# A chunked-attention and feed-forward kernel on one core: whole weight blocks staged in later weights' places, rests formed by TensorE, the first tile in one pass, and values and scores in one block

## The chip, the core and the metric

The kernel runs on one core of a Trainium2 chip. A core has five engines with an instruction queue each: PE (TensorE, matrix products, with its weight loads shown apart as PEld), DVE (VectorE), ACT (ScalarE), POOL (GpSimd) and SP (SyncE, which here only issues DMAs). Each queue runs strictly in the order in which the program emits instructions. Semaphores make one engine wait for another. The metric is the device time of one launch in microseconds (us); lower is better.

## What is computed

Eight batches of 576 tokens, eight heads of 64. Attention stays inside chunks of 64 tokens; then a normalised feed-forward block (FFN) with 2048 hidden units is added to its own input.

```python
scores = scale * np.matmul(q_c, k_c.transpose(0, 1, 2, 4, 3))     # chunks of 64
scores = scores - np.max(scores, axis=-1, keepdims=True)
attn = np.exp(scores); attn = attn / (np.sum(attn, axis=-1, keepdims=True) + 1e-09)
out = np.matmul(attn, v_c)                                         # -> x, 4608 tokens x 512
xn = (x - mu) / np.sqrt(var + 1e-06) * g_ln
ch = np.maximum(xn @ w_ch1, 0.0) @ w_ch2
return (x + ch).astype(np.float32)
```

The two FFN weight matrices come in as float64 and are converted on the chip.

## The kernel before

**Tiles and blocks.** The 4608 tokens are 18 pairs of 256 tokens, and 9 tiles of two pairs. The hidden units are 16 blocks f of 128. A block's weights are 128x1024: 512 columns for the first matrix and 512 rows of the second. For near-float32 accuracy every operand is held as a high part in the one-pass format fp32r (names ending in h) and a rest (names ending in l), and every product is three matmuls: high by high, high by rest, rest by high. `up(f)` (L287) is 12 matmuls 128x512 into the PSUM tile h for a whole tile (128x256 for a single pair); `split(f, h)` (L300) lets ACT form hh (L304) and DVE hl (L305); `down(f)` (L310) is 12 matmuls 128x512 for a tile (6 for a pair) that add into the four PSUM banks y. `finish` (L322) scales y, adds x (DVE, L326) and stores.

**Weight conversion.** `convert_w` (L116) runs over 32 half blocks of 512 columns. `fetch_w` (L78) loads a half block as 64-bit words (512 KB) into one of three buffers. `start_w` (L85) takes the absolute value of the high words into wf (ACT, L89). `round_w` (L92) packs float64 into float32 bits by four DVE instructions (L96, L97, L100, L104) and lets ACT round the result to the high part wh (L108). `split_w` (L110) forms the rest wl on DVE (L113), after which the buffer takes the next half.

**Attention of a pair** (L132): q and k by DMA, 64 small score matmuls (L159), row maxima (DVE, L166), subtraction (DVE, L172) and exponential (ACT, L176) into p_sb, transposes of p_sb, the sums of the rows (DVE, L182 to L184), 64 small value matmuls (L216), division into x (DVE, L224), mean and variance (L234, L235), xg (L239), transposes of xg, and the split of the transposed xg into xth and xtl. The pairs of the first two tiles do their transposes on PE (L191, L255), with ACT copying pt_sb and xth out of PSUM (L193, L256) and DVE forming xtl (L248). Later pairs transpose on DVE (L204, L267), with ACT forming xth (L270) and POOL forming xtl (L248).

**Order.** Everything above is a generator; a string names, letter by letter, which one takes its next step, and the engines' queues follow that order. START: a, b, A, B are the attentions of the pairs of tiles 0 and 1, C, D and E those of tile 2 and of the first pair of tile 3, w the conversion, and u/1, v/2, x/3, s/4 the products and splits of four single pairs (tiles 0 and 1) over blocks 0 to 5; y/5 and z/6 run blocks 6 to 15 of tiles 0 and 1 at full width. Then STEADY is played once for each of tiles 2 to 7 (FFN of one tile, u/1, beside the attention of the next one's pairs, A from its third step and B) and LAST for tile 8. In STEADY every block of 64 score or 64 value matmuls stands alone between FFN products. PSUM has eight banks: two for attention (`ps_a`), two for h, four for y.

Of the kernel before, what the change touches and what calls it, by code (L numbers as in the profile page):

```python
# [30 lines left out]
RAW_AHEAD = 3  # L31
# [4 lines left out]
START = "aawawaawawabwabAawawaabbwawaubbuwb11buwubu1BuAb1AAuwuAb1buwbAbAwvA2vAv2Auv1BwA2vvCu2vwBvu2vvwB12vAvB2AABBx3BwxBx3xBx3xB3xBwBBxx3x3CxDswxs34ws4sssw4s4sssw4w4swy5s4wyy5yw5ywyy5yywy5yyw5yw5ywC5yyw5wyCzCyw5C6yyzzC5CC6EzCC6CCzCCDzzz6zCD6Dzz6DDzD6zzDzzDD6DD6zzDzDD6z6D"  # L36

FIRST_FFNS = [("u1", 0, 0, 1, 0, 6), ("v2", 0, 1, 1, 0, 6), ("x3", 1, 0, 1, 0, 6), ("s4", 1, 1, 1, 0, 6), ("y5", 0, 0, 2, 6, 16), ("z6", 1, 0, 2, 6, 16)]
STEADY = "Au1ABu1AuAu1AuAu1AuAu1AuAu1AuAu1AuAu1AuBu1BEuBu1BuBu1BuBu1BuBu1BuBu1BuBu1BuBu1uu1"
LAST = "u1u1uu1uu1uu1uu1uu1uu1uu1uu1uu1uu1uu1uu1uu1uu1uu1"  # L40
# [10 lines left out]
def chunk_attention_ffn(ctx: ExitStack, tc: tile.TileContext, qkv, g, w, out):  # L51
# [10 lines left out]
    raw_pool = ctx.enter_context(tc.tile_pool(name="raws", bufs=RAW_AHEAD))  # L62
    ps_a = ctx.enter_context(tc.tile_pool(name="ps_a", bufs=2, space=PSUM))
# [4 lines left out]
    make_identity(nc, ident)  # L68
    mhalf = const.tile([P, 2], F32, name="mhalf")
# [3 lines left out]
    wh = [const.tile([P, NW], F32R, name=f"wh{i}") for i in range(NF)]  # L73
    wl = [const.tile([P, NW], F32R, name=f"wl{i}") for i in range(NF)]

    stage, converted = {}, set()

    def fetch_w(i):  # L78
        if i < 2 * NF:
            raw = raw_pool.tile([P, HALF], U64, name="raw")  # L80
            nc.sync.dma_start(raw, w[i // 2, :, (i % 2) * HALF : (i % 2 + 1) * HALF])
            words = raw.bitcast(U32).rearrange("p (n two) -> p n two", two=2)
            stage[i] = words[:, :, 0], words[:, :, 1]

    def start_w(i):  # L85
        if i < 2 * NF:
            lo, hi = stage[i]
            wf = raw_pool.tile([P, HALF], F32, name="wf", bufs=1)
            nc.scalar.activation(wf, hi.bitcast(F32), AF.Abs)  # L89
            stage[i] = lo, hi, wf  # L90

    def round_w(i):  # L92
# [10 lines left out]
        start_w(i + 1)  # L103
# [3 lines left out]
        f, cs = i // 2, slice((i % 2) * HALF, (i % 2 + 1) * HALF)  # L107
        nc.scalar.copy(wh[f][:, cs], lo.bitcast(F32))  # L108

    def split_w(i):  # L110
        wf = stage.pop(i)[0].bitcast(F32)
        f, cs = i // 2, slice((i % 2) * HALF, (i % 2 + 1) * HALF)
        nc.vector.tensor_tensor(out=wl[f][:, cs], in0=wf, in1=wh[f][:, cs].bitcast(F32), op=ALU.subtract)  # L113
        converted.add(i)

    def convert_w():  # L116

        for i in range(RAW_AHEAD):
            fetch_w(i)
        yield  # L120
        start_w(0)
        yield
        for i in range(2 * NF):
            round_w(i)
            if i > 0:
                split_w(i - 1)
                fetch_w(i - 1 + RAW_AHEAD)
            yield
        split_w(2 * NF - 1)
        yield  # L130

    def attention(pair, xt_cols, xs, by_pe):  # L132
# [8 lines left out]
        top = small.tile([P, 2 * HP, 2], F32, name="top")  # L141
        den = small.tile([P, 2 * HP, 2], F32, name="den")
        rden = small.tile([P, 2 * HP, 2], F32, name="rden")
        p_sb = work.tile([P, 2 * HP, 2, D], F32, name="p_sb", tag="work")

        def bank():
            return ps_a.tile([P, DM], F32, name="s")

        def rows(bank_):
            return bank_.rearrange("p (a d) -> p a d", d=D)  # L150

        s = [rows(bank()) for _ in range(2)]
# [10 lines left out]
        if by_pe:  # L163
            yield
        for h2 in range(2):
            nc.vector.tensor_reduce(out=top[:, :, h2], in_=s[h2], axis=AX.X, op=ALU.max)  # L166
# [4 lines left out]
        for h2 in range(2):  # L171
            nc.vector.tensor_tensor(  # L172
                out=p_sb[:, :, h2, :], in0=s[h2], in1=top[:, :, h2 : h2 + 1].broadcast_to([P, 2 * HP, D]),
                op=ALU.subtract,
            )
            nc.scalar.activation(p_sb[:, :, h2, :], p_sb[:, :, h2, :], AF.Exp, scale=scale)  # L176
            if by_pe and h2 == 0:
                yield
        yield

        def denominators():
            nc.vector.tensor_reduce(out=den, in_=p_sb, axis=AX.X, op=ALU.add)  # L182
            nc.vector.tensor_scalar_add(den, den, 1e-9)
            nc.vector.reciprocal(rden, den)  # L184


        pt_sb = work.tile([P, 2 * HP, 2, D], F32, name="pt_sb", tag="work")
        if by_pe:
            pt = [bank().rearrange("p (a t) -> p a t", a=HP) for _ in range(2)]
            for a in range(2 * HP):  # L190
                nc.tensor.transpose(out=pt[a // HP][:, a % HP, :], in_=p_sb[:, a, :, :], identity=ident)  # L191
            for j in range(2):
                nc.scalar.copy(  # L193
                    pt_sb[:, j * HP : (j + 1) * HP], pt[j].rearrange("p a (c t) -> p a c t", c=2)
                )
            yield
            denominators()
            yield
        else:
# [8 lines left out]
            denominators()  # L208

        o = [rows(bank()) for _ in range(2)]  # L210
        for j in range(2):
            for a in range(HP):
                for h2 in range(2):
                    r = slice(h2 * D, (h2 + 1) * D)
                    for c in range(2):
                        nc.tensor.matmul(  # L216
                            o[h2][c * D : (c + 1) * D, j * HP + a, :], lhsT=pt_sb[r, j * HP + a, c, :],
                            rhs=v_t[j][r, a, c, :], start=True, stop=True,
                        )
        yield  # L220
        x = keep.tile([P, 2, DM], F32, name="x")
        x_h = x.rearrange("p j (a b d) -> p (j a) b d", a=HP, b=2)
        for h2 in range(2):
            nc.vector.tensor_tensor(  # L224
                out=x_h[:, :, h2, :], in0=o[h2], in1=rden[:, :, h2 : h2 + 1].broadcast_to([P, 2 * HP, D]),
                op=ALU.mult,
            )
        yield
# [16 lines left out]

        def rest(on, j, xt):
            js = slice(j * P, (j + 1) * P)
            on.tensor_tensor(out=xtl[:, :, js], in0=xt, in1=xth[:, :, js].bitcast(F32), op=ALU.subtract)  # L248

        if by_pe:  # L250
            xt = []
            for j in range(2):
                xt.append(bank().rearrange("p (k t) -> p k t", k=NK))
                for k in range(NK):
                    nc.tensor.transpose(out=xt[j][:, k, :], in_=xg[:, j, k * P : (k + 1) * P], identity=ident)  # L255
                nc.scalar.copy(xth[:, :, j * P : (j + 1) * P], xt[j])  # L256
                if j == 0:
                    yield
                    rest(nc.vector, 0, xt[0])
            yield  # L260
            rest(nc.vector, 1, xt[1])
        else:
# [6 lines left out]
            for j in range(2):  # L269
                nc.scalar.copy(xth[:, :, j * P : (j + 1) * P], xt[:, j * NK : (j + 1) * NK, :])  # L270
                rest(nc.gpsimd, j, xt[:, j * NK : (j + 1) * NK, :])
# [7 lines left out]
    def ffn(first, n, xt, xs, fs, last):  # L279

        nt = n * PAIR
        slots = DM // nt
        held = []
        f0, f1 = fs
        y = []

        def up(f):  # L287
            assert 2 * f in converted and all(first + i in xs for i in range(n))
# [3 lines left out]
            for k in range(NK):  # L292
                for wx, x in ((wh, xth), (wh, xtl), (wl, xth)):
                    nc.tensor.matmul(  # L294
                        h, lhsT=wx[f][:, k * P : (k + 1) * P], rhs=x[:, k, :], start=m == 0, stop=m == 3 * NK - 1
                    )
                    m += 1
            return h

        def split(f, h):  # L300
            if f % slots == 0:
                held[:] = [hp_.tile([P, slots, nt], F32R, name=f"h{i}") for i in "hl"]
            hh, hl = (x[:, f % slots, :] for x in held)
# [4 lines left out]
            return hh, hl  # L308

        def down(f, hh, hl):  # L310
            assert 2 * f + 1 in converted
            if f == f0:
                y.extend(ps_y.tile([P, DM], F32, name="y") for _ in range(2 * n))
            for j in range(2 * n):
                js = slice(j * P, (j + 1) * P)
                for m, (hx, wx) in enumerate(((hh, wh), (hh, wl), (hl, wh))):
                    nc.tensor.matmul(  # L317
                        y[j], lhsT=hx[:, js], rhs=wx[f][:, DM:],
                        start=f == f0 and m == 0, stop=f == f1 - 1 and m == 2,
                    )  # L320

        def finish():  # L322
            for j in range(2 * n):
                pair, jj = first + j // 2, j % 2
                x, rstd = xs[pair]
                nc.vector.scalar_tensor_tensor(  # L326
# [104 lines left out]
```

## Time and profile before

| | us |
|---|---|
| median of 3 runs | 898.54 (897.41 to 898.60) |
| profiled execution | 899.33 |
| its span on the core | 897.60 |
| granted TensorE clock | 0.997 |
| busy: PE, DVE, ACT | 853.5, 568.3, 173.3 |

The span is what the instruction rows cover; the profiled execution's own time is 1.73 us longer, and 0.79 us above the median of the runs. In all rows the first number of a timeline or chain line is the start in us from the beginning of the span and the second its duration. Matmuls overlap, so the distance between the starts of two neighbours is what one costs, not the duration that its row shows. The chain of waits goes backwards from the last instruction and names at each step what was waited for.

### The profile page before, as it was taken

To read this page: it belongs to the slowest core of one execution; us is meant where nothing else is said; L and a number is where in the kernel's file an instruction comes from. 1 tells how busy PE (TensorE), PEld (TensorE's weight loads), DVE (VectorE), ACT (ScalarE), POOL (GpSimd) and SP (SyncE) were. 2 spreads that over 40 slices of the span, in tenths; PEclk is the share of its full clock that TensorE was granted. 3 is DMA by queue.
4 is the path that set the end of the run, shared out by engine and by line. 5 is a ranking of instruction groups with operands and counts; after the bars stand their busy time and mean duration, and the time that the engine had idled before them with its cause. 6 is when DMAs were issued, how large, how long until landed. Compare 5 with 4: busy or idle time off the path is not lost.

```text
span 897.6 us, 14036 instructions
## 1 busy us (share of the span) xinstructions
PE 853.5 (95%) x5968; PEld 706.5 (79%) x5968; DVE 568.3 (63%) x1104; ACT 173.3 (19%) x301; POOL 48.3 (5%) x53
## 2 busy tenths in 40 slices
PE   2379999999999999999999999999999999999998
PEld 2368888888888788878888888888888888888886
DVE  5988887788876566656565656565666565661112
ACT  3343433412111111121212021212011111111110
POOL 0000000001000000010101010101010101010000
PEclk9999999999999999999999999999999999999999
DMA  6544153212030103010301030103010220000001
GB/s 220 191 145 161 62 175 118 94 48 71 1 135 8 48 0 119 24 47 1 119 24 47 1 118 24 47 1 117 25 47 1 72 71 1 1 30 19 0 1 47
DMA packets 20367, 55.70 MB, mean 62 GB/s; under 512 B 2256, under 2 KB 2256, under 8 KB 20304
## 3 DMA queue, kind: packets, MB, share of 16 engines
q1 hardware_dynamic: 20160, 54.53, 17.4%
q8 instruction: 47, 0.77, 0.4%
q10 hardware_dynamic: 144, 0.26, 0.1%
q14 instruction: 16, 0.13, 0.0%
HBM read 45.35 MB, written 9.44 MB: 61 GB/s over the span
## 4 chain that ended last, share of the span: by engine, by line
PE 89%; DVE 6%; DMA 2%; ACT 1%; issue 1%; SPq 0%; DVEq 0%; ACTq 0%
PE h L294 44%; PE y L317 41%; PE s L159 2%; PE s L216 2%; DMA k_t<-qkv 1%; DVE pt_sb L204 1%; DMA raw<-w 1%; DVE raw L100 1%; DVE raw L104 1%; DVE x L326 1%; DVE hl L305 1%; ACT hh L304 1%; DVE wf L97 0%; DVE top L166 0%; DVE wl L113 0%
## 5 line engine op out<-in xcount | busy, mean ns | idle before, releaser
L305 DVE SCALAR_TENSOR_TENSOR hl<-h,hh 128x512 fp32r<-128x512 f32 (+1 forms) x156 | 101.2, 650 | 264.8 <-ACT hh L304 264.6
L294 PE MATMUL h<-xth,wh 128*128 128x512 f32 (+1 forms) x624 | 236.6, 379 | 0.7 <-ACT xth L256 0.7
L294 PE MATMUL h<-xth,wl 128*128 128x512 f32 (+1 forms) x624 | 233.9, 375 | 3.0 <-DVE wl L113 3.0
L294 PE MATMUL h<-xtl,wh 128*128 128x512 f32 (+1 forms) x624 | 234.0, 375 | 1.1 <-DVE xtl L248 1.1
L317 PE MATMUL y<-wh,hh 128*128 128x512 f32 x576 | 226.0, 392 | 2.1 <-ACT hh L304 2.0
L317 PE MATMUL y<-wl,hh 128*128 128x512 f32 x576 | 224.4, 390 | 0.0
L317 PE MATMUL y<-wh,hl 128*128 128x512 f32 x576 | 224.4, 390 | 0.0
L304 ACT ACTIVATE hh<-h 128x512 fp32r<-128x512 f32 (+1 forms) x156 | 87.8, 564 | 582.5 <-PE h L294 578.9
L294 PEld LDWEIGHTS h<-xth,wl 128*128 128x128 f32 x624 | 118.6, 190 | 23.9 <-DVE wl L113 3.2
L294 PEld LDWEIGHTS h<-xth,wh 128*128 128x128 f32 x624 | 118.5, 190 | 23.2 <-ACT xth L256 1.1
L294 PEld LDWEIGHTS h<-xtl,wh 128*128 128x128 f32 x624 | 118.5, 190 | 22.0 <-DVE xtl L248 1.4
L317 PEld LDWEIGHTS y<-wh,hh 128*128 128x128 f32 x576 | 108.2, 188 | 25.1 <-ACT hh L304 3.0
L317 PEld LDWEIGHTS y<-wh,hl 128*128 128x128 f32 x576 | 108.1, 188 | 23.4 <-DVE hl L305 0.9
L317 PEld LDWEIGHTS y<-wl,hh 128*128 128x128 f32 x576 | 108.2, 188 | 21.5
L204 DVE STREAM_TRANSPOSE pt_sb<-p_sb 32x256 f32<-32x256 f32 x224 | 97.7, 436 | 5.2 <-ACT p_sb L176 1.4
L267 DVE STREAM_TRANSPOSE xt<-xg 32x256 f32<-32x256 f32 x224 | 97.6, 436 | 3.5
L248 POOL TENSOR_TENSOR xtl<-xt,xth 128x512 fp32r<-128x512 f32 x28 | 35.6, 1290 | 644.8 <-ACT xth L270 416.0
L326 DVE SCALAR_TENSOR_TENSOR x<-y,rstd,x 128x512 f32<-128x512 f32 x44 | 30.6, 749 | 15.3 <-PE y L317 15.2
L166 DVE TENSOR_REDUCE top<-s 128x8 f32<-128x512 f32 x36 | 23.2, 686 | 24.4 <-PE s L159 24.4
L89 ACT ACTIVATE wf<-raw 128x512 f32<-128x512 f32 x32 | 21.8, 683 | 76.5 <-DMA raw<-w 53.8
L159 PE MATMUL s<-k_t,q_t 64*64 64x64 f32 x1152 | 22.6, 231 | 14.1 <-DMA k_t<-qkv 14.1
L159 PEld LDWEIGHTS s<-k_t,q_t 64*64 64x64 f32 x1152 | 20.0, 144 | 19.2 <-issue 11.1
(35 smaller groups left out, 383.7 us busy)
## 6 DMA issues: line engine op xcount, KB each, us to landing
raw<-w SPq DMA_DIRECT2D x32, 512.0 KB, 3.6
q_t<-qkv SPq DMA_DIRECT2D x18, 512.0 KB, 4.2
k_t<-qkv SPq DMA_DIRECT2D x18, 512.0 KB, 5.4
v_t<-qkv SPq DMA_DIRECT2D x36, 256.0 KB, 3.1
out<-x SPq DMA_DIRECT2D x36, 256.0 KB, 2.1
g_sb<-g ACTq DMA_DIRECT2D x1, 256.0 KB, 4.5
```

The costliest lines, as they stand in the source:

```text
L89: nc.scalar.activation(wf, hi.bitcast(F32), AF.Abs)
L159: nc.tensor.matmul(s[h2][c * D : (c + 1) * D, j * HP + a, :], lhsT=q_t[r, a, cs], rhs=k_t[r, a, cs], start=True, stop=True,)
L166: nc.vector.tensor_reduce(out=top[:, :, h2], in_=s[h2], axis=AX.X, op=ALU.max)
L204: nc.vector.transpose(out=pt_sb[quad(2 * h2 + j), :, c, quad(i)], in_=p_sb[quad(2 * c + i), :, h2, quad(j)])
L216: nc.tensor.matmul(o[h2][c * D : (c + 1) * D, j * HP + a, :], lhsT=pt_sb[r, j * HP + a, c, :], rhs=v_t[j][r, a, c, :], start=True, stop=True,)
L248: on.tensor_tensor(out=xtl[:, :, js], in0=xt, in1=xth[:, :, js].bitcast(F32), op=ALU.subtract)
L267: nc.vector.transpose(out=xt[quad(j), :, quad(i)], in_=xg[quad(i), :, quad(j)])
L294: nc.tensor.matmul(h, lhsT=wx[f][:, k * P : (k + 1) * P], rhs=x[:, k, :], start=m == 0, stop=m == 3 * NK - 1)
L304: nc.scalar.activation(hh, h, AF.Relu)
L305: nc.vector.scalar_tensor_tensor(out=hl, in0=h, scalar=0.0, in1=hh.bitcast(F32), op0=ALU.max, op1=ALU.subtract)
L317: nc.tensor.matmul(y[j], lhsT=hx[:, js], rhs=wx[f][:, DM:], start=f == f0 and m == 0, stop=f == f1 - 1 and m == 2,)
L326: nc.vector.scalar_tensor_tensor(out=x[:, jj, :], in0=y[j], scalar=rstd[:, jj : jj + 1], in1=x[:, jj, :], op0=ALU.mult, op1=ALU.add)
```

## The change

- Weights: 17 units in place of 32. Block 0 is still converted in halves (units 0 and 1), every other block as a whole (1024 columns, 1 MB by DMA). A whole block needs a bigger buffer: three of them serve, one of its own (`raw`) and the places in which the converted weights of blocks 14 and 15 will stand (`places`). The packing is cut in three steps (`round_w`, `split_w` of the unit before, `sign_w`). For the first four units (blocks 0 to 2) the rest is formed by TensorE: identity times the float32 value plus minus-identity times the high part, in y banks that are still unused, copied out by ACT.
- Attention: the two banks of `ps_a` are one tile; maxima, subtraction, exponential and division each become one instruction over 1024 columns. Pairs a and b get the sums of their rows from TensorE (64 one-column matmuls among the value matmuls, L275 of the new kernel). For the first two tiles the rest xtl is minus-identity times xth added onto the transposes in PSUM, copied by ACT. For later pairs the value products go to the two h banks instead.
- Order: the first tile is finished before the second begins its FFN. Pairs 0 and 1 run blocks 0 to 5 singly, then tile 0 runs blocks 6 to 15. STEADY is played for tiles 1 to 7. In STEADY the values of one pair and the scores of the next stand together (`AB` and `BE` in the string), at two places for a tile; `ROOM = (3, 11)` names the blocks before which no further `up` is emitted, so that both h banks are free for the values there. In the last tile the last two blocks' `down` are ordered by bank of y.

The core of the diff:

```diff
-START = "aawawaawawabwabAawawaabbwawaubbuwb11buwubu1BuAb1AAuwuAb1buwbAbAwvA2vAv2Auv1BwA2vvCu2vwBvu2vvwB12vAvB2AABBx3BwxBx3xBx3xB3xBwBBxx3x3CxDswxs34ws4sssw4s4sssw4w4swy5s4wyy5yw5ywyy5yywy5yyw5yw5ywC5yyw5wyCzCyw5C6yyzzC5CC6EzCC6CCzCCDzzz6zCD6Dzz6DDzD6zzDzzDD6DD6zzDzDD6z6D"
-STEADY = "Au1ABu1AuAu1AuAu1AuAu1AuAu1AuAu1AuAu1AuBu1BEuBu1BuBu1BuBu1BuBu1BuBu1BuBu1BuBu1uu1"
+START = "aawwwwaawwwwwwawbwawwawbwbabwwaawaaawwbwwuA1wbbu1uwuwuAuB1Awubu1u1Awbwuu1bbbbuwvwAvw22AwAAvvvvB2EwA2wvv2vABvy2w3yBvwAww3vAyAwwywwyw3yA3BwyBwByByByBw3wB3wyByBww3yyBwwyEw3wywyy33yy3"
+STEADY = "ABu1Au1AuAu1AuAu1AuABuAu1AEu1AuAu1AuAu1AuAu1BuBu1BuBu1BuBu1BuBEuBBu1BBu1BuBBu1Buu1uu1"
+SINGLE = 6
+BY_PE = 4
+ROOM = (3, 11)
...
+    places = {f: ("raw", f"w{NF - 1}", f"w{NF - 2}")[f % 3] for f in range(NF - 2)}
+    places.update({NF - 3: f"w{NF - 2}", NF - 2: f"w{NF - 1}", NF - 1: "raw"})
...
+        if i < BY_PE:
+            for j in range(wf.shape[1] // HALF):
+                js = slice(j * HALF, (j + 1) * HALF)
+                z = sums(1)[j % 2]
+                nc.tensor.matmul(z, lhsT=ident, rhs=wf[:, js], start=True, stop=False)
+                nc.tensor.matmul(z, lhsT=minus, rhs=wh[:, js], start=False, stop=True)
+                nc.scalar.copy(wl[:, js], z)
+        else:
+            nc.vector.tensor_tensor(out=wl, in0=wf, in1=wh.bitcast(F32), op=ALU.subtract)
...
+        fetch_w(0)
+        yield
+        start_w(0)
+        for i in range(1, 4):
+            fetch_w(i)
+            yield
+        for i in range(units):
+            round_w(i)
+            yield
+            start_w(i + 1)
+            if i > 0:
+                split_w(i - 1)
+            if i > 1:
+                fetch_w(i + 2)
+            yield
+            sign_w(i)
+            yield
...
+        if by_pe:
+            o2 = banks()
+            o = [o2[:, h2, :] for h2 in range(2)]
+        else:
+            o = [ps_h.tile([P, DM], F32, name="h") for _ in range(2)]
...
+                        if den_by_pe:
+                            nc.tensor.matmul(
+                                dens[h2][cs, ja : ja + 1], lhsT=lhsT, rhs=ones[r, 0:1], start=True, stop=True
+                            )
...
+                nc.tensor.matmul(
+                    xt[:, j, :], lhsT=minus, rhs=xth[:, :, js], start=False, stop=True, skip_group_check=True
+                )
+                nc.scalar.copy(xtl[:, :, js], xt[:, j, :].rearrange("p (k t) -> p k t", k=NK))
...
+            ups = iter(range(f0, f1))
+            for f in range(f0, f1):
+                for _ in range((f not in room) + (f == f0 or f - 1 in room or tail and f == NF - 3)):
+                    i = next(ups, None)
+                    if i is not None:
+                        up(i)
+                        yield
...
-        for t in range(2, NTILE):
-            now.update(zip("u1", tiles[t].ffn(0, 2, (0, NF), True)))
+        for t in range(1, NTILE):
+            now.update(zip("u1", tiles[t].ffn(0, 2, room=ROOM if t + 1 < NTILE else ())))
```

More of the change, by code (lines that the diff above doesn't have):

```diff
@@ L102, in round_w, with sign_w @@
         )
-        start_w(i + 1)
+    def sign_w(i):
+        lo, hi, _ = stage[i]
         nc.vector.scalar_tensor_tensor(
@@ L140, in attention, with banks, rows @@
         scale = 1.0 / float(D) ** 0.5
[L141 to L152, printed above, removed]
+        groups = 2 * HP
+        def banks():
+            return ps_a.tile([P, 2, DM], F32, name="s")
+        def rows(bank):
+            return bank.rearrange("p (a d) -> p a d", d=D)
+        s2 = banks()
+        s = [rows(s2[:, h2, :]) for h2 in range(2)]
         for j in range(2):
@@ L162, in attention @@
                         )
[L163 to L166, printed above, removed]
+        yield
+        top = small.tile([P, 2, groups], F32, name="top")
+        s4 = s2.rearrange("p b (a d) -> p b a d", d=D)
+        nc.vector.tensor_reduce(out=top, in_=s4, axis=AX.X, op=ALU.max)
         v_t = [load.tile([P, HP, 2, D], F32, name="v_t", bufs=2) for _ in range(2)]
@@ L170, in attention @@
         yield
[L171 to L178, printed above, removed]
-        yield
[L181 to L187, printed above, removed]
+        p_sb = work.tile([P, groups, 2, D], F32, name="p_sb", tag="work")
+        nc.vector.tensor_tensor(
+            out=p_sb.rearrange("p a b d -> p b a d"), in0=s4,
+            in1=top.rearrange("p b (a one) -> p b a one", one=1).broadcast_to([P, 2, groups, D]), op=ALU.subtract,
+        )
+        nc.scalar.activation(p_sb, p_sb, AF.Exp, scale=scale)
+        yield
+        pt_sb = work.tile([P, groups, 2, D], F32, name="pt_sb", tag="work")
         if by_pe:
-            pt = [bank().rearrange("p (a t) -> p a t", a=HP) for _ in range(2)]
-            for a in range(2 * HP):
-                nc.tensor.transpose(out=pt[a // HP][:, a % HP, :], in_=p_sb[:, a, :, :], identity=ident)
+            pt = banks().rearrange("p j (a t) -> p j a t", a=HP)
+            for a in range(groups):
+                nc.tensor.transpose(out=pt[:, a // HP, a % HP, :], in_=p_sb[:, a, :, :], identity=ident)
             for j in range(2):
                 nc.scalar.copy(
-                    pt_sb[:, j * HP : (j + 1) * HP], pt[j].rearrange("p a (c t) -> p a c t", c=2)
+                    pt_sb[:, j * HP : (j + 1) * HP], pt[:, j].rearrange("p a (c t) -> p a c t", c=2)
                 )
-            yield
-            denominators()
             yield
@@ L207, in attention @@
                     yield
-            denominators()
-        o = [rows(bank()) for _ in range(2)]
+        den = small.tile([P, groups, 2], F32, name="den")
+        rden = small.tile([P, groups, 2], F32, name="rden")
+        if not den_by_pe:
+            nc.vector.tensor_reduce(out=den, in_=p_sb, axis=AX.X, op=ALU.add)
+            nc.vector.tensor_scalar_add(den, den, 1e-9)
+            nc.vector.reciprocal(rden, den)
+            yield
[4 more added lines that the diff above has]
+            o = [ps_h.tile([P, DM], F32, name="h") for _ in range(2)]
+        dens = sums(pair) if den_by_pe else None
+        if den_by_pe:
+            assert pair not in taken
+            taken.add(pair)
         for j in range(2):
@@ L277, in attention, with ffn @@
         yield
-    def ffn(first, n, xt, xs, fs, last):
-        nt = n * PAIR
+    def ffn(pairs, xt, xs, f0, f1, room=()):
+        nt = len(pairs) * PAIR
         slots = DM // nt
-        held = []
-        f0, f1 = fs
-        y = []
+        hs, held = {}, []
+        tail = pairs[-1] == NPAIR - 1
         def up(f):
-            assert 2 * f in converted and all(first + i in xs for i in range(n))
+            assert 2 * f in converted and all(pair in xs for pair in pairs)
             h = ps_h.tile([P, nt], F32, name="h")
@@ L307, in split, with down @@
             )
-            return hh, hl
-        def down(f, hh, hl):
+            hs[f] = hh, hl
+        def down(f, j):
             assert 2 * f + 1 in converted
[L312 to L326, printed above, removed]
-                    out=x[:, jj, :], in0=y[j], scalar=rstd[:, jj : jj + 1], in1=x[:, jj, :], op0=ALU.mult, op1=ALU.add
-                )
-                if last:
-                    row = pair * PAIR + jj * P
-                    nc.sync.dma_start(out[row : row + P, :], x[:, jj, :])
-        hs = {}
+            taken.add(pairs[j // 2])
@@ new lines, in down, with finish @@
+            hh, hl = (x[:, j * P : (j + 1) * P] for x in hs[f])
+            wh, wl = (x[:, DM:] for x in weights(f))
+            for m, (hx, wx) in enumerate(((hh, wh), (hh, wl), (hl, wh))):
+                nc.tensor.matmul(
+                    sums(pairs[j // 2])[j % 2], lhsT=hx, rhs=wx,
+                    start=f == 0 and m == 0, stop=f == NF - 1 and m == 2,
+                )
+        def finish(j):
+            pair, jj = pairs[j // 2], j % 2
+            x, rstd = xs[pair]
+            nc.vector.scalar_tensor_tensor(
+                out=x[:, jj, :], in0=sums(pair)[jj], scalar=rstd[:, jj : jj + 1], in1=x[:, jj, :],
+                op0=ALU.mult, op1=ALU.add,
+            )
+            row = pair * PAIR + jj * P
+            nc.sync.dma_start(out[row : row + P, :], x[:, jj, :])
@@ L335, in products @@
+        count = 2 * len(pairs)
+        done = []
         def products():
-            hs[f0] = up(f0)
-            yield
+            ups = iter(range(f0, f1))
             for f in range(f0, f1):
-                if f + 1 < f1:
-                    hs[f + 1] = up(f + 1)
-                    yield
-                down(f, *hs.pop(f))
-                hs["done"] = f + 1
+                for _ in range((f not in room) + (f == f0 or f - 1 in room or tail and f == NF - 3)):
+                    i = next(ups, None)
+                    if i is not None:
+                        up(i)
+                        yield
+                if tail and f >= NF - 2:
+                    continue
+                for j in range(count):
+                    down(f, j)
+                done.append(f)
+                yield
+            if tail:
+                for j in range(count):
+                    for f in range(NF - 2, NF):
+                        down(f, j)
+                done.append(NF - 1)
@@ L347, in rectified @@
             for f in range(f0, f1):
-                hs[f] = split(f, hs[f])
+                assert f < f0 + 2 or f - 2 in done
+                split(f)
                 yield
-            assert hs["done"] == f1
-            finish()
-            yield
+            if f1 == NF:
+                assert NF - 1 in done
+                for j in range(count):
+                    finish(j)
+                yield
         return products(), rectified()
```

151 lines of the change are left out of this document (91 added, 60 removed).

## The prediction, made before the changed kernel ran

> **What bounds the kernel now.** I read the busy shares first, then the slices, a table by stage, and the chain of waits.
>
> ```profile
> PE 853.5 (95%) x5968; PEld 706.5 (79%) x5968; DVE 568.3 (63%) x1104; ACT 173.3 (19%) x301; POOL 48.3 (5%) x53
> ...
> PE   2379999999999999999999999999999999999998
> ...
> DVE  5988887788876566656565656565666565661112
> ```
>
> ```profile
> 0.00:40.00 40.00, 11.14 (x209) 9.02 (x209) 29.16 (x53) 13.46 (x21) 0.74 (x7) 1.00 0.59 217
> 40.00:250.00 210.00, 200.81 (x1600) 170.44 (x1601) 174.67 (x337) 66.08 (x120) 8.99 (x10) 0.99 0.28 99
> 250.00:807.00 557.00, 554.99 (x3779) 455.74 (x3778) 350.36 (x696) 84.19 (x144) 38.56 (x37) 1.00 0.13 44
> 807.00:897.60 90.60, 86.52 (x382) 71.34 (x380) 14.10 (x21) 9.57 (x16) 0.00 (x0) 0.99 0.05 20
> ```
>
> The columns of the table are the stretch, then busy us of PE, PEld, DVE, ACT and POOL, the clock, the DMA share and GB/s. From 250 us on PE is busy 555.0 of 557.0 us: only fewer or denser products help there. In the first 40 us PE works 11.1 us and DVE 29.2: that is the loss. The chain of waits shows the period of a steady tile, the first product of tile 2, and how the opening goes:
>
> ```profile
> 1.17 5.25 DMA k_t<-qkv
> ...
> 6.56 1.99 PE s L159 x64
> ...
> 17.68 6.73 DMA k_t<-qkv
> ...
> 27.50 5.53 DMA raw<-w
> ...
> 40.87 2.71 PE h L294 x11
> ```
>
> ```profile
> 249.77 5.67 PE h L294 x24
> ...
> 293.21 2.95 PE h L294 x12
> ...
> 386.18 2.95 PE h L294 x12
> ```
>
> FFN products flow from 40.87 us, after two late loads (k of the second pair, a weight half whose buffer came free late). A steady tile takes 386.18 - 293.21 = 92.97 us. START, with tiles 0 and 1, ends about 249.8 us. So the time is START + 6 tiles + the last tile + the tail.
>
> **The change, part 1: values and scores together.** Two neighbouring places of one steady tile, start and duration:
>
> ```profile
> 291.73 0.39 PE L317 MATMUL y<-wh,hl 128*128 128x512 f32 x1
> 292.05 1.16 PE L159 MATMUL s<-k_t,q_t 64*64 64x64 f32 x64
> 293.14 0.50 PE L294 MATMUL h<-xth,wh 128*128 128x512 f32 x1
> 293.48 0.39 PE L294 MATMUL h<-xtl,wh 128*128 128x512 f32 x1
> ```
>
> ```profile
> 309.37 0.39 PE L317 MATMUL y<-wh,hl 128*128 128x512 f32 x1
> 309.69 0.34 PE L216 MATMUL s<-v_t,pt_sb 64*64 64x64 f32 x6
> 310.36 1.14 PE L216 MATMUL s<-v_t,pt_sb 64*64 64x64 f32 x58 [0.33 <-DVE pt_sb L204]
> 311.44 0.50 PE L294 MATMUL h<-xth,wh 128*128 128x512 f32 x1
> 311.77 0.40 PE L294 MATMUL h<-xtl,wh 128*128 128x512 f32 x1
> ```
>
> A full matmul costs 0.2267 us (2.72 us for 12), so a tile's 384 cost 87.04. From 291.73 to 293.48 there lie two of them and 1.30 us: 64 small matmuls in 1.09 (292.05 to 293.14, 17 ns each) and 0.21 of changing over. The second place costs 1.95, since its values wait on DVE's transposes (0.33 us shown, and a second start). Four places, three at 1.30 and one at 1.95, make 5.85; 92.97 - 87.04 = 5.93 agrees. After: two places of 128 small matmuls at 2 x 1.09 + 0.21 = 2.39, so a tile takes 87.04 + 4.78 = **91.82 us**, 1.15 less, if nothing new waits. Between 2.39 and two separate 1.30 the place has no other price, so the upper bound is +0.42 for a tile.
>
> Does something wait? The values now come after `den` in DVE's order, behind four transposes and one split. Adding the DVE instructions by the new string, the transposes end near 15.8 us of the tile, split and sums near 19.3; PE reaches the values at 19.0 and needs only transposes and splits (17.7). They go to the h banks: the banks are free once hl of blocks 2 and 3 is done (17.7 too). Behind the values stand the scores (1.1) and `down(3)` (2.7), which cover DVE's two divisions (1.3) before `up(4)` wants the bank. The second place is alike (DVE 63.7, PE 65.2). The margin is 1.3 us; if DVE falls behind by more, PE waits at 14 places.
>
> **Part 2: the sum after START.** The steady string is now played 7 times, once more than before, and START shrinks to tile 0. The last tile keeps 87.04, the tail its rows:
>
> ```profile
> 891.60 2.76 DVE L326 SCALAR_TENSOR_TENSOR x<-y,rstd,x 128x512 f32<-128x512 f32 x4 [2.16 <-PE y L317]
> ...
> 893.13 0.39 PE L317 MATMUL y<-wh,hl 128*128 128x512 f32 x1
> ```
>
> DVE's last scaling ends at 894.36 in either order, since it waits for the last bank; I give the new order nothing (0 to 0.3 us). From the last matmul's slot (893.36) to 897.60 are 4.24 us. After START: 7 x 91.82 + 87.04 + 4.24 = **734.0 us**.
>
> **Part 3: START.** DVE's prices:
>
> ```profile
> 119.43 0.42 DVE L96 TENSOR_SCALAR wf<-wf 128x512 f32<-128x512 f32 x1
> ...
> 121.67 0.69 DVE L113 TENSOR_TENSOR wl<-raw,wh 128x512 fp32r<-128x512 f32 x1
> ```
>
> ```profile
> L182 DVE TENSOR_REDUCE den<-p_sb 128x16 f32<-128x1024 f32 x18 | 21.8, 1213 | 0.2
> ...
> L305 DVE SCALAR_TENSOR_TENSOR hl<-h,hh 128x512 fp32r<-128x512 f32 x132 | 91.3, 692 | 253.7 <-ACT hh L304 253.5
> ...
> L305 DVE SCALAR_TENSOR_TENSOR hl<-h,hh 128x256 fp32r<-128x256 f32 x24 | 9.9, 420 | 11.1 <-ACT hh L304 11.1
> ```
>
> A half unit's five instructions take 2.9 us (119.43 to 121.67, and the last). From 256 to 512 columns an instruction grows by 0.27 us, so 1024 columns take about 1.2, as L182 does. A whole block then costs 0.7 + 0.7 + 1.25 (round), 1.15 (sign) and 1.15 (rest): 5.0 in place of 5.8; for three blocks the rest leaves DVE. All weights: 77 us (before 32 x 2.9 = 92). Four pairs of attention at 7.3 to 8.4: 31. Splits and finish: 13. **DVE in START: 121 us.**
>
> PE in START: FFN of tile 0, 12 half-width `up` at 1.44, 12 half `down` at 1.36, 10 full blocks at 5.44: 88.0. Five score and four value places at 1.3: 11.7, row sums 2.2 (64 one-column matmuls each, priced as scores), transposes 12.4, xtl 1.8, and six rest pairs. **PE in START: 123 us.** Their rows:
>
> ```profile
> 41.25 0.41 PE L294 MATMUL h<-xth,wl 128*128 128x256 f32 x1
> 41.46 0.41 PE L294 MATMUL h<-xth,wh 128*128 128x256 f32 x1
> ...
> 45.80 0.28 PE L294 MATMUL h<-xtl,wh 128*128 128x256 f32 x1
> 45.92 0.28 PE L294 MATMUL h<-xth,wl 128*128 128x256 f32 x1
> ```
>
> ```profile
> 32.69 1.09 PE L255 MATMUL s<-ident,xg 128*128 128x128 f32 x4 [6.15 <-DVE p_sb L172]
> ...
> 64.20 0.60 PE L255 MATMUL s<-ident,xg 128*128 128x128 f32 x4
> ```
>
> The same 128x256 product is spaced 0.21 us at 41.3 and 0.12 at 45.9: PE runs at half speed until it has been busy for some 4.5 us. No row has a float32 matmul of 512 columns. The nearest are four float32 transposes: 0.60 when PE is warm, 1.09 cold; the fp32r one is 0.23 warm, 0.45 cold. A rest pair is bounded by 0.45 and 1.5; I take the cold end, since it comes before 40 us, 1.1 in the sum. The Trainium skill, FP8 and Floating Point Precision, section TensorE Precision Notes, says that a true float32 product takes four passes, which speaks against this use of TensorE: an estimate by it is 0.91 us warm and 1.8 cold for 512 columns, so a cold pair would be 2.3, and my sum would rise by about 1.5 us through the one place below that waits for two pairs. No run here shows it yet.
>
> *The opening.* The new string puts ahead of the first product all attention of pair a, pair b up to its exponential, and units 0 to 6 up to rounding: 33.4 us of DVE work, 16.7 of PE. DVE begins at 8.57 as before (the first scores are unchanged). Loads are no longer what is late:
>
> ```profile
> 2.00:6.00 4.00, 0.00 (x0) 1.00 0.98 353
> 6.00:10.00 4.00, 1.99 (x64) 1.00 1.01 387
> ```
>
> The queue moves 0.35 to 0.39 MB a us when it has work. Behind a's q and k (1 MB) now stand 3 MB of weights, then v, then b's q and k: v lands near 16 us and b's near 19; before, b's landed at 24.4. New waits: a's values sit behind the rests of units 0 and 1 on PE and the copies on ACT (about 20 to 24.5 us), b's scores behind unit 2's two rest pairs (to about 30), and DVE, whose next instruction is b's maximum, stands for 3 to 4 us. 8.6 + 33.4 + 3.7 puts DVE at 45.7 when it has done unit 6's round; the last of a's xtl copies on ACT and b's transposes on PE let the first product start at about **45 us**, 4 later than before, with six blocks rounded. Before, there were three and a half: the table by stage for the wl line (L113) shows 7 halves up to 45 us.
>
> ```profile
> 0.00:45.00 45.00, 4.79 (x7) 1.00 0.56 205
> ```
>
> *The rest.* From there PE has 123 - 17 = 106 us left, DVE 121 - 33 = 88. So DVE, which by the slices was about as busy as PE up to 135 us before, gets ahead and PE flows. PE's losses: 2.3 us cold, and the in-order waits that I find by laying the two sums beside each other (`down5` on hl5 behind a whole block's round, b's transposes on xg): 2 to 3. START ends at 45 + 106 + 4.5 = **155.5 us**. Bounds: 149 (opening at 40 and no waits), 166 (below).
>
> Sum: 155.5 + 734.0 = 889.5 us of span, 891.2 with the 1.73 outside it; the median of the runs stood 0.8 below the profiled execution, so **890.4**. About 0.2% (1.8 us) is what a measurement of this kernel can tell from no change.
>
> **Rivals.**
> - *Quicker opening* (16%): DVE's stop for b's maximum is covered and the first product comes at 40. For it: loads are in time. START 149, total 884.
> - *The h banks stall PE* (13%): the division or a late split holds `up(4)` or the values. For it: 1.3 us of margin only, and DVE's order is rigid. 14 places at 0.5 to 0.7 us take 7 to 10 us: 897 to 900, half of it within 0.2%.
> - *Slower: the opening is stretched by whole blocks* (18%). Every attention step of the four pairs uses the one two-bank tile, and each hop waits for an instruction that may stand behind 2.7 us of a round in place of 1.6, and behind copies on ACT. Six hops before the first product at 1.9 us more: it starts at 56, START ends at 167, total 902. It decides from the point at which the first product comes after 53 us. Against it: ACT was busy only 13.5 of the first 40 us. In 15 of these 18 the time is over 900.3.
> - Forecast (53%): 886 to 895.
>
> **The numbers.** Faster by over 0.2%: 53 + 16 + half of 13, 76%; within: 9%; slower: 15%. The range, 882 to 900, leaves out most of the slower rival and a little below.
>
> **What would show it.** Steady period 91.8 with two gaps of 2.4; no PE wait on x, hl or pt_sb there. First product near 45, tile 1's first near 155. DVE with idle time before 155. It is wrong if the period is 92.5 or more, or the first product comes after 53.

## The result, and the profile after

| | before | after |
|---|---|---|
| median, 4 runs each | 898.57 (897.41 to 899.25) | 883.94 (882.32 to 885.38) |
| profiled execution / its span | 899.33 / 897.60 | 884.80 / 883.00 |

The ratio is 0.9838 (95% interval 0.9816 to 0.9860): 14.6 us faster, where 8.2 were forecast. The sum was made against the span, so I compare it there: 889.5 predicted, 883.0 measured. First the busy shares, and PE's and DVE's slices of the changed kernel:

```profile
PE 856.3 (97%) x6050; PEld 706.4 (80%) x6050; DVE 538.3 (61%) x963; ACT 173.6 (20%) x262; POOL 50.6 (6%) x54
...
PE   4699999999999999999999999999999999999998
...
DVE  5988885657575666567656766666566657661112
```

The table by stage of the changed kernel (stretch, busy us of PE, PEld, DVE, ACT and POOL, clock, DMA share, GB/s):

```profile
40.00:150.00 110.00, 107.03 (x951) 90.98 (x952) 86.22 (x116) 46.97 (x66) 3.98 (x3) 0.96 0.38 135
...
250.00:790.00 540.00, 540.00 (x3741) 447.16 (x3740) 342.19 (x666) 81.29 (x130) 38.28 (x36) 1.00 0.12 41
```

From 250 us PE is now busy for the whole stretch (before, 555.0 of 557.0), and from 40 to 150 us it stands for 3 us only. The first 40 us are still the loss (the first two slices of PE). The chain of waits of the changed kernel gives the terms of the sum:

```profile
42.24 2.56 PE h L369 x12
...
151.95 5.44 PE h L369 x24
...
221.74 5.44 PE h L369 x24
...
243.50 5.44 PE h L369 x24
...
313.28 5.44 PE h L369 x24
...
701.23 5.44 PE h L369 x24
...
791.84 5.44 PE h L369 x24
```

42.24 is the first FFN product. 151.95, 243.50, 701.23 and 791.84 are the first products of tile 1, of tile 2, of tile 7 and of the last tile. 221.74 and 313.28 are the same place of two neighbouring tiles: the period is 91.54 us.

| term | predicted | measured | difference |
|---|---|---|---|
| first product | 45 | 42.24 | -2.8 |
| from there to tile 1 | 110.5 | 109.71 | -0.8 |
| six steady tiles (701.23 - 151.95) | 550.92 | 549.28 | -1.6 |
| the seventh (791.84 - 701.23) | 91.82 | 90.61 | -1.2 |
| last tile and tail | 91.28 | 91.16 | -0.1 |
| span | 889.5 | 883.0 | -6.5 |

Against the kernel before, the same frame is tile 2's first product: 249.77 before, 243.50 after. START (with tile 1) gave 6.3 us and all behind it 8.3 (647.83 to 639.50).

**The steady tile.** The chain at one joined place of the changed kernel (start, duration, engine, tile, line):

```profile
168.27 2.72 PE y L389 x12
170.99 1.09 PE h L271 x64
172.08 0.93 PE s L206 x64
173.01 2.95 PE y L389 x12
```

The values (L271) take 1.09 as before, the scores right behind them 0.93, and the next FFN block 2.95 in place of 2.72, which is the change-over: 2.25 in all. The tile is 87.04 + 2 x 2.25 = 91.54. DVE at the same place (timeline; in brackets its own idle time and what ended it):

```profile
168.94 0.69 DVE L378 SCALAR_TENSOR_TENSOR hl<-h,hh 128x512 fp32r<-128x512 f32 x1 [1.05 <-ACT hh L377]
169.55 1.21 DVE L249 TENSOR_REDUCE den<-p_sb 128x16 f32<-128x1024 f32 x1
...
172.12 1.29 DVE L294 TENSOR_TENSOR x<-h,rden 128x512 f32<-128x512 f32 x2 [0.86 <-PE h L271]
```

DVE waits for PE here and not the other way: the sums of the rows are done before the values are, and the two divisions end at 173.41, beside the scores and `down(3)`.

**START.** What PE waited for between its first FFN product and 152 us (total, times, longest), before:

```profile
PE s L191 <- DVE xtl L248: 3.0, 2, 1.9
PE h L294 <- DVE wl L113: 3.0, 1, 3.0
PE y L317 <- ACT hh L304: 2.0, 3, 0.9
PE h L294 <- DVE xtl L248: 1.1, 1, 1.1
```

and in the changed kernel from 42.2 us to its end:

```profile
PE s L321 <- ACT xth L324: 0.7, 1, 0.7
PE s L328 <- ACT xth L324: 0.7, 1, 0.7
PE s L328 <- ACT xtl L331: 0.7, 1, 0.7
PE s L231 <- ACT xtl L331: 0.7, 1, 0.7
```

9.1 us of waits have become 2.8. The wait on a weight rest (wl) is gone, and with it the waits on hh and on xtl by DVE; what is left are hops between PE and ACT. So START's 6.3 us came from the stretch behind the first product: the first product itself is 1.4 us later than before (40.87), and from there to tile 2's first product it takes 201.26 us in place of 208.90. In this stretch PE's idle time fell from 8.3 to 2.7 us by the table of busy time, and its work from 200.6 to 198.6, of which 0.8 are tile 1's two joined places (priced below). What of the change took these waits away, the experiments below test only in part.

### The profile page after: what moved, and what is told of

Its sections match the earlier page's. It is cut to its first block, busy times and chain, and to the rows that moved or that the text cites. A ratio compares the mean times of both kernels' runs of the same rounds, so it can differ in the third digit from the quotient of the medians.

```text
span 883.0 us, 13918 instructions
## 1 busy us (share of the span) xinstructions
PE 856.3 (97%) x6050; PEld 706.4 (80%) x6050; DVE 538.3 (61%) x963; ACT 173.6 (20%) x262; POOL 50.6 (6%) x54
## 4 chain that ended last, share of the span: by engine, by line
PE 97%; DVE 1%; issue 1%; ACT 1%; DMA 1%; SPq 0%
PE y L389 45%; PE h L369 45%; PE s L206 2%; PE h L271 2%; PE s L231 1%; DMA k_t<-qkv 1%; PE y L144 1%; PE s L271 1%; PE s L321 0%; PE s L328 0%; ACT xtl L331 0%; ACT xth L324 0%; PE y L275 0%; DVE raw L123 0%; DVE top L213 0%
## 5 line engine op out<-in xcount | busy, mean ns | idle before, releaser
L369 PE MATMUL h<-xth,wp 128*128 128x512 f32 (+1 forms) x1200 | 379.3, 382 | 0.0
L389 PE MATMUL y<-wp,hh 128*128 128x512 f32 x1152 | 358.1, 392 | 0.0
L369 PEld LDWEIGHTS h<-xth,wp 128*128 128x128 f32 x1200 | 224.0, 189 | 43.5
L389 PEld LDWEIGHTS y<-wp,hh 128*128 128x128 f32 x1152 | 214.8, 188 | 44.7 <-ACT hh L377 0.2
L369 PE MATMUL h<-xtl,wp 128*128 128x512 f32 (+1 forms) x600 | 228.9, 381 | 0.0
L389 PE MATMUL y<-wp,hl 128*128 128x512 f32 x576 | 224.9, 390 | 0.0
L369 PEld LDWEIGHTS h<-xtl,wp 128*128 128x128 f32 x600 | 113.3, 189 | 21.9
L389 PEld LDWEIGHTS y<-wp,hl 128*128 128x128 f32 x576 | 108.4, 188 | 23.2 <-DVE hl L378 0.4
L309 DVE SCALAR_TENSOR_TENSOR xg<-x,mv,g_sb 128x512 f32<-128x512 f32 x36 | 25.3, 743 | 0.0
L304 DVE BATCH_NORM_STATS2 stats<-x 128x6 f32<-128x512 f32 x36 | 24.3, 675 | 0.3
```

What stands on the lines that cost most here:

```text
L304: nc.vector.bn_stats(out=stats, in_=x[:, j, :])
L309: nc.vector.scalar_tensor_tensor(out=xg[:, j, :], in0=x[:, j, :], scalar=mv[:, j, 0:1], in1=g_sb, op0=ALU.subtract, op1=ALU.mult)
L369: nc.tensor.matmul(h, lhsT=wx, rhs=x[:, k, :], start=m == 0, stop=m == 3 * NK - 1)
L389: nc.tensor.matmul(sums(pairs[j // 2])[j % 2], lhsT=hx, rhs=wx, start=f == 0 and m == 0, stop=f == NF - 1 and m == 2,)
```

## The experiments

Each kernel is the changed one with one edit, except the two that are marked as the kernel before. A ratio is against the kernel before, timed on the same chip (898.77, 898.64 and 898.61 us in the three groups). For the steady tile my theory was that joining saves time at each place by itself, and the rival that only the removed wait counts. For START the theory was that the time of the first product sets the end; against it stood that the lead in converted weights decides, and that PE's own work bounds START while DVE has slack.

**The changed kernel once more**, as the mark for the others.

> The changed kernel once more, so that the others of this call have it beside them on one chip. Expected 882 to 886 us, ratio to before 0.982 to 0.986, a steady tile of 91.54 us, the first FFN product at 42.2 us and the first product of tile 1 at 152.0 us as in its first profile. If these move by more than 1 us from run to run, differences of that size between kernels mean nothing.

882.58 us (881.98 to 884.46), ratio 0.9819 (0.9805 to 0.9833). In its profile START ends at 151.54 and the period is 91.55.

**Values and scores apart.** Same two places, one FFN product between the two blocks:

```diff
-STEADY = "ABu1Au1AuAu1AuAu1AuABuAu1A...BuBEuBBu1BBu1BuBBu1Buu1uu1"
+STEADY = "ABu1Au1AuAu1AuAu1AuAuBAu1A...BuBuEBBu1BBu1BuBBu1Buu1uu1"
```

> Only the steady string differs from the changed kernel: each block of 64 score matmuls comes one FFN product after the 64 value matmuls in place of right behind them (13 such places). Theory A, joining itself saves time: a place of its own costs 1.30 us as before, two of them 2.60 against 2.25 joined, so a tile takes 92.2 us and the kernel is about 4.6 us slower than the changed one (888 to 889). By the prediction's own price (0.21 a place) it would be 2.7 us slower. Rival B, the steady gain is only the vanished wait on the transposes (0.65 a tile of before): no difference, 884.

889.47 us (886.87 to 889.98), ratio 0.9886 (0.9871 to 0.9902). The chain at the same place as above:

```profile
168.03 1.09 PE h L271 x64
169.12 2.95 PE y L389 x12
172.06 1.09 PE s L206 x64
```

The scores are back at 1.09, and each block has a change-over of its own (2.95 behind the values). The period is 92.32, 0.78 more, so a joined place saves 0.39 us: 0.16 in the second block and 0.23 of change-over. At 13 places that is 5.1 us, and the two profiles agree: from the first product of tile 1 to the end it takes 736.1 us (885.1 - 148.99) against 731.05. The medians differ by 6.9, since the granted clock was 0.990 in three of the four runs with the blocks apart and 0.994 in three of the four of the changed kernel, and it moves START's end (last section). Between runs of equal clock the difference is 3.8 to 5.5 us.

**The waiting place alone, in the kernel before.** Two tries, since the first moved the wrong one:

```diff
-STEADY = "Au1ABu1AuAu1AuAu1AuAu1A...BuBu1BEuBu1BuBu1BuBu1BuBu1..."
+STEADY = "Au1ABu1AuAu1AuAu1uAAu1A...BuBu1BEuBu1BuBu1BuBu1BuBu1..."   # first try: pair A
+STEADY = "Au1ABu1AuAu1AuAu1AuAu1A...BuBu1BEuBu1BuBu1Buu1BBuBu1..."   # second: pair B
```

> The kernel before, with one thing changed in its steady string: the value products of the first pair stand one FFN product later, so that the transposes are done when TensorE gets there. Theory A: the 0.65 us of the place that waits go in each of 6 tiles; a tile takes 92.3 us in place of 92.97 and the kernel 894.7, 3.9 less. Rival: something else is late at the new place (the division right behind it on VectorE, then the split of the hidden block), and the tile stays at 93.

898.73 us, ratio 1.0000 (0.9991 to 1.0009). A miss of the edit: pair A's values did not wait. The place that did is pair B's, unchanged in its chain:

```profile
309.63 0.45 DVE pt_sb L204
...
310.12 1.14 PE s L216 x58
```

> The kernel before, with pair B's value products (the place that waited on DVE's transposes, 0.65 us above its three neighbours) one FFN product later in STEADY. Theory: the wait is a matter of order alone, so it goes in all 6 steady tiles, the period falls from 92.97 to about 92.3 and the time by 6 x 0.65 = 3.9 us, to about 894.7. Together with the 0.39 us for each joined place (two of them in a tile, 0.78) that would make up the 1.43 us by which the changed kernel's period is shorter. Rival: DVE's later work only shifts and the wait turns up at the next place or on hl; the period stays near 93.0 and the time at 898.6.

894.71 us (894.29 to 896.27), ratio 0.9957 (0.9943 to 0.9971), as the theory had it. The chain:

```profile
292.39 2.95 PE h L294 x12
...
311.66 1.09 PE s L216 x64
...
384.71 1.36 PE h L294 x5
```

No DVE step stands ahead of the values any more, and the period is 92.32 (384.71 - 292.39), 0.65 less. So one letter moved in the old order gives 3.9 of the 14.6 us. With two joined places at 0.39 the steady account closes: 92.97 - 0.65 - 0.78 = 91.54.

**Values into the attention banks, not the h banks.**

```diff
-            o = [ps_h.tile([P, DM], F32, name="h") for _ in range(2)]
+            o = [o2[:, h2, :] for h2 in range(2)]     # o2 = banks() for every pair
```

> The changed kernel, but the value products of later pairs go to the two attention banks in place of the h banks; order and strings as they are. The scores right behind them must then wait until VectorE has divided the values out of these banks. Theory: TensorE stands 1.4 to 1.6 us at each of 13 joined places, 18 to 21 us in all (901 to 904), slower than before. Rival: the h banks bought nothing, 883.

904.38 us (903.90 to 904.71), ratio 1.0061 (1.0047 to 1.0074), slower than the kernel before. PE's longest waits and the chain at a place:

```profile
PE s L206 <- issue: 20.3, 14, 1.5
```

```profile
168.44 1.14 PE s L268 x64
169.58 1.41 issue
170.99 1.16 PE s L206 x64
172.15 2.95 PE y L386 x12
```

The profile names no releaser ("issue"), but the times fit: the scores want the two banks that DVE's division still reads, DVE's timeline has the division from 169.60 to 170.89, and the scores start at 170.99. PE stands 1.41 us between the blocks. The h banks, with `ROOM` that empties them, are what lets the joined place work.

**Pair a and the first product earlier.** Pair a's attention is pulled ahead of the weights in START:

```diff
-"...awbwawwawbwbabwwaawaaawwbwwuA1wbbu1uwuwuAuB1Awub..."
+"...awbwawaaaawaaawbwbub1wuwuwbw1uwuwbwAwbwwAuB1Awub..."
```

> Only the first letters of START differ from the changed kernel: the division, statistics, scaling and transposes of the first pair come right behind its values, ahead of the second pair's scores and of the weight blocks 2 and later, and the first FFN products follow at once. Theory A, the time of the first FFN product sets the end of START: it comes at 32 to 35 us in place of 42.2, and the kernel is 4 to 8 us faster than the changed one (876 to 880). Rival B, VectorE's total of START (some 121 us of work, now with the second pair's attention later) sets it: TensorE stands between products before 100 us for as long as it gained, and the time stays within 2 us of 884.

890.16 us (889.12 to 891.88), ratio 0.9901 (0.9886 to 0.9915). The first product came at 36.2 us, 6 earlier, and START ended at 157.2, more than 5 later. The table by stage of this kernel:

```profile
30.00:40.00 10.00, 9.73 (x98) 6.56 (x98) 2.45 (x2) 5.16 (x8) 0.18 (x1) 0.76 0.38 136
40.00:60.00 20.00, 11.35 (x230) 9.13 (x228) 18.75 (x24) 9.43 (x13) 0.00 (x0) 0.88 0.61 223
```

and its chain at the loss:

```profile
48.19 1.14 DVE wp L148
...
49.38 0.33 SPq L104
...
50.90 6.99 DMA k_t<-qkv
```

DVE did 2.45 us of work from 30 to 40: pair b's maximum waited 6.68 us for its scores, which now stand on PE behind rests of weights. PE stood 8.65 of the next 20. The chain shows why: a load of k is queued on SP behind a weight fetch (L104) that waits for its buffer, which DVE frees with the rest of an earlier block (L148). This one load is 6.1 us of PE's waiting; on a converted weight PE waited 0.9. Both forecasts missed. An earlier first product does not bring an earlier end when a load behind it comes late; a shortage of converted weights hardly shows.

**The rests off TensorE.** First the weight rests (`BY_PE = 0`), then xtl of the first two tiles (DVE subtracts from PSUM), then both:

```diff
-BY_PE = 4
+BY_PE = 0
...
-                nc.tensor.matmul(
-                    xt[:, j, :], lhsT=minus, rhs=xth[:, :, js], start=False, stop=True, skip_group_check=True
+                nc.vector.tensor_tensor(
+                    out=xtl[:, :, js], in0=xt[:, j, :].rearrange("p (k t) -> p k t", k=NK),
+                    in1=xth[:, :, js].bitcast(F32), op=ALU.subtract,
                 )
-                nc.scalar.copy(xtl[:, :, js], xt[:, j, :].rearrange("p (k t) -> p k t", k=NK))
```

> The changed kernel, but all rests of the weights by VectorE, none by TensorE (three blocks, 3.5 us more of VectorE work, nearly all ahead of the first FFN product). Theory A: VectorE's work ahead of the first product delays it one for one and nothing else changes, so START ends 2 to 3.5 us later and the kernel takes 884.5 to 886. Rival: the rest products and their copies on ScalarE hold up the second pair's scores and the transposes of the first by more than VectorE saves (by four passes a product, 2.3 us a cold pair): then the kernel gets faster without them, 880 to 882.

> The changed kernel, but the rest xtl of the first two tiles is formed by VectorE out of PSUM, as before, in place of a product with minus identity and a copy by ScalarE. It takes two cold products and two copies out of the chain ahead of the first product (37.3 to 40.2 us), and puts 1.3 us of VectorE work and a wait for ScalarE's copies ahead of the sixth unit's rounding. Theory A: the first product comes 1 to 2 us earlier, VectorE's later work 2 to 3 us later, the sum within 2 us of the changed kernel (882 to 886). Rival: the chain is what counts, 880 to 881.

> The changed kernel with no rest formed by TensorE: the rests of the first four weight units and of xtl in the first two tiles are all subtracted by DVE. PE loses some 6 us of products (four pairs of 128x512 and two single ones are 0.5 us or more each, and eight transposed halves), DVE gains some 9 us. If PE alone bounds START, its end comes up to 4 us earlier than about 151.5 and the time falls to 879 to 881. If DVE's lead in the opening counts, the first product comes 2 to 3 us later as it did with the weight rests alone on DVE, START ends at 151 to 154 and the time is 882 to 885, no different from the changed kernel.

Without weight rests on PE 884.56 (ratio 0.9840, 0.9827 to 0.9853), without xtl 882.09 (0.9823, 0.9804 to 0.9842), without both 884.20 (0.9845, 0.9826 to 0.9864). None differs from the changed kernel by more than its runs scatter; the medians point to up to 2 us for the weight rests and to none for xtl. The first 42 us in the table by stage, changed kernel:

```profile
0.00:42.00 42.00, 21.78 (x301) 14.06 (x301) 30.47 (x41) 21.26 (x28) 1.98 (x9) 0.88 0.67 244
```

and with both rests on DVE:

```profile
0.00:42.00 42.00, 13.26 (x279) 11.74 (x280) 30.86 (x44) 16.43 (x19) 1.98 (x9) 1.00 0.62 232
```

PE lost 8.5 us of work in a stretch in which it is idle about half the time, and START ended at 151.14 against 151.95. In these medians, which engine forms the rests is close to free. That the weight rests on PE gain nothing does not follow: with them on DVE the first product came at 44.24, 2.0 us later, and yet START ended at 151.29, but at a granted clock of 1.00 from 42 to 80 us where the changed kernel had 0.90. Beside the same START at 0.97 and 0.99 (last section) it ends about 2 us later, by as much as its first product. With xtl alone on DVE the first product came 1.8 us earlier, but PE then waited 4.5 us behind it in place of 2.8, and START ended at 149.13, like the same START at that clock. These are single profiles.

**Whole blocks in halves.** Every conversion instruction over 1024 columns is cut into two over 512; staging, order and DMAs stay.

```diff
-            nc.scalar.activation(wf, hi.bitcast(F32), AF.Abs)
+            for wf_, hi_ in cut(wf, hi):
+                nc.scalar.activation(wf_, hi_.bitcast(F32), AF.Abs)
```

> The changed kernel, but every conversion instruction on VectorE and ScalarE works on 512 columns, two in place of one for a whole block; loads, buffers and order stay. VectorE gets about 0.75 us more for each of 15 blocks, 11 us in START, some 4 of it ahead of the first product. Theory A (work ahead of the first product delays one for one, later work has slack): 886 to 888. Rival B (VectorE's total sets the end of START): 890 to 894. Rival C (the prediction's sum taken literally, TensorE alone bounds): 883 to 884.

883.59 us (883.36 to 885.96), ratio 0.9835 (0.9821 to 0.9848): no difference from the changed kernel, and the number of the theory that PE alone bounds. DVE's busy time from 120 to 140 us grew from 15.11 to 18.13 with PE busy throughout. Behind the first product DVE has the slack to take the smaller instructions. Ahead of it they may cost about 1 us: the first product came at 43.12 (42.24 and 41.82 in the two profiles of the changed kernel) and START ended at 153.08 (151.95 and 151.54). The medians cannot tell that.

## Why the prediction was right or wrong

The direction, the places and the mechanism of the steady tile were right; three terms were mis-sized, all to the same side. The time lies inside the stated range, but below the main forecast of 886 to 895.

- *Joined places.* "Two places of 128 small matmuls at 2 x 1.09 + 0.21 = 2.39" counted a saved change-over and nothing else. Measured is 2.25: the second block of 64 runs in 0.93 us behind another of its kind. No row before showed two such blocks in a row, so 1.09 was the right row to take, and the lower side of its bound was missing: I had bounded the place upward only. This is 2.0 us over the seven tiles. That the removed wait counts 0.65 a tile and that nothing new waits both hold (the kernel before with pair B's values later; no PE wait in the steady tiles).
- *The seventh steady tile.* "7 x 91.82" gave it scores at its second place. It prepares no tile after the last one, so its second place is values alone: 90.61 measured. Of the 1.2 us some 0.9 are this miscount. The chain before had it already, in the tile ahead of the last (91.87 us, where the others take 92.97):

```profile
714.61 5.67 PE h L294 x24
...
806.48 5.44 PE h L294 x24
```

- *The opening.* That DVE "stands for 3 to 4 us" at pair b's maximum failed. DVE's timeline of the changed kernel:

```profile
26.33 1.22 DVE L213 TENSOR_REDUCE top<-s 128x16 f32<-128x1024 f32 x1 [0.37 <-PE s L206]
```

 The stop was 0.37 us, because PE gave the scores by 26.3 and not by 30. This is what the rival "quicker opening" said, but the first product came at 42.24 and not at its 40. The reason is in the last steps ahead of the first product in the chain of the changed kernel:

```profile
32.90 1.14 ACT wf L112
34.04 0.96 ACT wp L146 x2
35.00 0.50 ACT xth L324
...
35.54 1.13 PE s L321 x4
...
39.63 0.59 ACT xtl L331
...
40.27 1.97 PE s L231 x8
```

 From 32.9 us the chain holds no DVE step: behind an absolute value and two weight copies on ACT, xth, xtl and the next pair's transposes pass seven times between ACT and PE, and that sets the first product. The prediction named a's copies and b's transposes as the last steps, but took the time from DVE's sum and gave the hops no duration. DVE ended unit 6's round at 44.03 (45.7 forecast), 1.8 us behind the first product, which did not wait for it: five blocks were rounded by then, not six.
- *From the first product on.* 106 us of work and 4.5 of losses were forecast; PE's busy time is 107.1 of 109.8. "Laying the two sums beside each other" was right in kind: the forecast DVE idle time is there, 86.2 busy of the 110 us from 40 to 150.
- *The estimate from the Trainium skill.* The Trainium skill, FP8 and Floating Point Precision, section TensorE Precision Notes, has a true float32 product take four passes; the estimate by it was 2.3 us for a cold pair, against my 1.1. The trace has the float32 product at 1.05 cold (last section); with 0.43 for its fp32r partner a cold pair is 1.48, the upper end of my own bounds and well below that estimate, so the trace does not agree with the four passes. At the place that would have waited, PE stood another 1.05 us between unit 2's two pairs and b's scores (23.88 to 24.93), so up to that much more would have been hidden there; no run tests it.
- *The slower rival* (whole blocks stretch the opening) fell at its own point: 42.24 is before 53 us. That *the h banks stall PE* did not happen at a margin of some 1.3 us; with the banks shared it does, at 1.41 us a place.

The time, 884, is the number that the quicker opening gave, but by luck: START ended at 152 and not at its 149, and all behind START took 731.1 us and not 734.0. Only 2.8 of the 6.5 us by which the sum was too high lie ahead of the first product.

**Still open.** Behind the first product PE waits 6.3 us less. The early-pair experiment shows that a late load costs it there; whether PE's waits went by the staging in three large buffers, by the order of START, or by finishing one tile before the next, was not separated, since the order is written for the staging. No experiment gave a version that is faster than the changed kernel by more than its runs scatter.

## What to carry to other kernels

A block of small matmuls among large ones pays for the change of shape beside its own work (0.39 of 1.30 us here): put blocks of the same shape side by side, if a spare PSUM bank lets the second start without the first one's reader. Look in a periodic schedule for the one place that differs from its like; here one letter was worth 3.9 us. In an opening, count the hops between engines on the last stretch, the lead of the loads and what each queue holds up, not the busy time of one engine: an earlier first product (by 6 us) made the kernel about 7 us slower.

## What the runs showed of the hardware that was not expected

**A float32 matmul of 512 columns** shows as two rows in the trace. Chunks of 512 columns, each followed by its fp32r partner (L145), in PE's timeline of the changed kernel:

```profile
13.68 2.04 PE L144 MATMUL y<-raw,ident 128*128 128x512 f32 x2 [4.89 <-issue]
14.73 1.42 PE L145 MATMUL y<-wp,minus 128*128 128x512 f32 x1
...
22.58 1.06 PE L144 MATMUL y<-raw,ident 128*128 128x512 f32 x2
23.06 0.81 PE L145 MATMUL y<-wp,minus 128*128 128x512 f32 x1
```

From the first start of the pair of rows to the start of the next line it takes 1.05 us at the start and 0.48 at 22.6 us. Cold against cold (0.43 for the fp32r product, six of them in 2.56 us from 67.10) and warm against warm (0.2267) that is a little over twice the fp32r product, not four times.

**The granted clock of the opening** went with PE's work in it. In all profiles with weight rests on PE (21 to 24 us busy in the first 42) it was 0.88 to 0.90 there; in the two without them (13.3 us busy) and in the kernel before (12.3) it was 1.00. A lower clock makes the same work longer, so part of the 21 us is its effect; the runs don't tell which came first.

**START's end moves by itself, with the granted clock.** From the first product to tile 1's first product, in the chain of each profile whose START differs from the changed kernel's in nothing or only ahead of 44 us or in the width of DVE's and ACT's instructions:

| profile | first product | tile 1's first | between | clock, 42 to 80 us |
|---|---|---|---|---|
| changed kernel | 42.24 | 151.95 | 109.71 | 0.90 |
| once more | 41.82 | 151.54 | 109.72 | 0.91 |
| whole blocks in halves | 43.12 | 153.08 | 109.96 | 0.89 |
| values into the attention banks | 41.77 | 149.40 | 107.63 | 0.97 |
| values and scores apart | 41.89 | 148.99 | 107.10 | 0.99 |
| weight rests on DVE | 44.24 | 151.29 | 107.05 | 1.00 |

The stretch takes 107.1 to 107.6 us at the higher clock and 109.7 to 110.0 at the lower, whenever it begins. PE's timeline has a place of it: behind the same hops between PE and ACT, six fp32r products took 2.56 us (from 67.10) in the changed kernel and 1.38 (from 65.37) in the one with the blocks apart. Why the same START meets one or the other is open. A difference of under 3 us in START is therefore settled only between profiles of equal clock, and of each there are few.
